# A fused attention and expert kernel: two rings for cluster scores, later casts, a later assignment for batch 1, and another bank in the opening

## The chip, the cores and the metric

The kernel runs on one core of a Trainium2 chip. The metric is the time of one execution on the device in microseconds (us); most executions agree within 0.3%. PE is the matrix engine, DVE the vector engine, ACT the scalar engine, POOL the engine called GpSimd, SP the engine whose queue issues most transfers. A profile is one execution; its span, from the first to the last instruction, is some 1.8 us shorter than the time.

## The reference, cut to what matters

```python
q_n, k_n, c_n = (x / (norm(x) + 1e-6) for x in (q, k, centroids))
q_assign = argmax(einsum('bhsd,hcd->bhsc', q_n, c_n), -1)     # 16 clusters a head
k_assign = argmax(einsum('bhsd,hcd->bhsc', k_n, c_n), -1)
mask = q_assign[:, :, :, None] == k_assign[:, :, None, :]
attn = softmax(where(mask, scale * q @ k.T, -1e9)) @ v         # (4, 8, 768, 64)
x = attn.transpose(0, 2, 1, 3).reshape(3072, 512)
p = domain_probs / (domain_probs.sum(-1, keepdims=True) + 1e-9)
for e in range(4):
    out += p[:, e:e+1] * (maximum(x @ w1[e], 0) @ w2[e])
```

Every query and every key of a head is assigned to its nearest cluster. A query attends to the keys of its own cluster. The result goes through four dense experts whose outputs are summed with weights.

## The kernel before: the parts that matter here

PE's instruction order is fixed by the program. Attention is cut into steps (24 to a unit of query rows, 72 to a batch), and the expert matmuls are woven between them. A third strand assigns the next batch to clusters: raw keys and queries are turned to have the head dimension on partitions, scored against the centroids, turned back, and the best cluster's one-hot row is written beside the keys and queries. This third strand is a list of numbered items, doled out over a stretch of steps, at most one item at each place where the experts yield.

```python
PS_BUFS = {"s": 2, "av": 1, "av2": 1, "mo": 3, "misc": 1}      # eight PSUM banks in rings
...
class Paced:                                   # items of a strand, spread over steps
    def run(self, step):
        if self.done < min(self.n, (step - self.at) * self.n / (self.to - self.at)):
            self.done += 1
            next(self.gen, None)
...
def assigns(b):                                # (keys, queries) of heads 0-3, then of heads 4-7
    xs = [Crossed(b, t, g, (("misc",), ("mo",))[t == 0])
          for t, g in ((1, 0), (0, 0), (1, 1), (0, 1))]
    for y, x in enumerate(xs):
        z = y % 2                              # 0: keys, 1: queries
        ...                                    # batch 1 is turned on PE, batches 2 and 3 by transfers
            put(t + 15, x.casts)               # DVE: fp32 to bf16 (t = 8 * y)
            at = 16 * (y // 2) + 24
        ...
        put(at, lambda x=x: x.scores_split("mo"))   # PE into "mo", then four DVE copies
...
# an expert: ph = bank("mo") four times (L728, emptied by ACT), then for each half of its rows
po = bank("mo")[:, c]                          # L747
nc.vector.scalar_tensor_tensor(oacc[:, c], po, pap, oacc[:, c], ...)   # L756, empties po
...
k1.turn(2, act)                                # the opening: last two turns of keys,
k1.turn(3, dve)                                # in "misc" and in "s" (attention's own ring)
...
at_step = {1: lambda: (puts(k0, 1), qa.put_narrow(slice(2, HG), "dve"), casts(k1, (1,))), ...}
...
for b in range(1, B):
    gens.append(Paced(assigns(b), XSTEPS[b], PER_B * (b - 1) if b > 1 else S1 + 4,   # S1 = 28
                      PER_B * b - 2))                                                # PER_B = 72
```

A tile takes a free bank of its ring, which is one whose last reader stands earlier in the program; PE then waits until that reader has run.

The softmax here doesn't subtract the row's maximum and nothing guards it: scores larger than these inputs give would overflow.

Of the kernel before, what the change touches and what calls it, by code (L numbers as in the profile page):

```python
# [20 lines left out]
def kernel(  # L21
# [27 lines left out]
    HG = H // 2  # L49
# [24 lines left out]
    act, dve, pool = nc.scalar.copy, nc.vector.tensor_copy, nc.gpsimd.tensor_copy  # L74
# [35 lines left out]
    def late(t, b):  # L110
        x = KF[b % 2].rearrange("p h r c -> p (h r c)")
        n = NP * A * 128
        return x[:, t * n:(t + 1) * n].rearrange("p (x i r c) -> p x i r c", i=QT, r=2, c=128)
# [28 lines left out]
    def load_raw(n=1, upto=len(ORDER)):  # L142
        for _ in range(n):
            if loaded < upto:
                load_part(*take_raw())

    def cast_v(b, g, js=range(HG)):
        for j in js:
            pool(VX[b % 2][:, g * HG + j, :, :D],
                 raw[b, 2, g][:, j, :].rearrange("p (a d) -> p a d", d=D))  # L150

    def load_w(e):
        nc.gpsimd.dma_start(out=W1[e], in_=moe_w1[e].rearrange("(i p) f -> p i f", p=128))
        nc.gpsimd.dma_start(out=W2[e], in_=moe_w2[e].rearrange("(i p) f -> p i f", p=128))
# [57 lines left out]
    class Assign:  # L212
# [104 lines left out]
        def put(self, j, r, on):  # L317

            p0 = 2 * CL * j
            self.move(self.rows(slice(D, D + CL), j, r),  # L320
                      self.ot[p0:p0 + CL, r * self.w:(r + 1) * self.w], on)
# [22 lines left out]
    class Crossed(Assign):  # L344
# [38 lines left out]
        def casts(self):  # L383
            y = self.g * HG // 2
            if self.b < ROWS:
                for r in range(2):
                    dve(self.rows(slice(0, D), slice(0, HG), r),
                        self.all[D * r:D * r + D, :].rearrange("p (j c) -> p j c", j=HG))
                return
            dve(late(self.t, self.b)[:, y:y + HG // 2], self.rows_of())  # L390
# [67 lines left out]
    def assigns(b):  # L458


        xs = [Crossed(b, t, g, (("misc",), ("mo",))[t == 0])
              for t, g in ((1, 0), (0, 0), (1, 1), (0, 1))]
        todo = {}

        def put(at, *fs):
            todo.setdefault(at, []).extend(fs)

        def turn(x, j):
            x.turn(j, dve)
            for r in range(2):  # L470
                x.cast(j, r, pool)

        for y, x in enumerate(xs):
            z = y % 2
            if b == 1:
                t = 12 * (y // 2) + 4 * z
                for j in range(HG):
                    put(t + j, lambda x=x, j=j: turn(x, j))
                put(t + 3, lambda: load_raw(upto=13))
                at = 12 * (y // 2) + 8  # L480
            else:
                t = 8 * y
                for j in range(HG):
                    put(t + j, lambda x=x, j=j: x.split(j))
                    put(t + 2 + j, lambda x=x, j=j: x.cross(j))
                    put(t + 9 + j, lambda x=x, j=j: x.merge(j))
                put(t + 6, load_raw)
                put(t + 15, x.casts)
                at = 16 * (y // 2) + 24
            if b == 1:  # L490
                put(at, lambda x=x: x.scores(dve))
                put(at + 1 + z, x.back, x.top, x.scale_onehot, x.cross_onehot)
                put(at + 4 + z, x.send_all)
                continue
            put(at, lambda x=x: x.scores_split("mo"))
            put(at + 2 + 6 * z, x.cross_scores)
            put(at + 5 + 6 * z, x.merge_scores)
            if b < ROWS:
                put(at + 9 + 6 * z, x.top, x.scale_onehot, x.cross_onehot)
                put(at + 13 + 6 * z, x.send_all)  # L500
                continue
            put(at + 9 + 6 * z, x.top, x.number, x.cross_numbers)
            put(at + 12 + 6 * z, x.store_numbers)
            put(at + 14 + 6 * z, x.spread_numbers)
        for g in range(2):
            if b == 1:
                put(1 + 18 * g, lambda g=g: load_w(2 + g))
                put(26 + 3 * g, lambda g=g: cast_v(b, g), lambda: load_raw(upto=13))
            else:
                for j in range(HG):  # L510
                    put(36 + 8 * g + j, lambda g=g, j=j: cast_v(b, g, (j,)))
                put(40 + 8 * g, load_raw)
        for at in range(XSTEPS[b]):
            for f in todo.pop(at, []):
                f()
            yield
        assert not todo
# [253 lines left out]
    PER_B = UB * PER_U  # L771
    LEAD = 6
    XSTEPS = [0, 31, 63, 63]
    step = 0
    gens = []
# [20 lines left out]
    k0, k1 = Assign(0, 1, 0, ("s", "mo", "mo", "mo")), Assign(0, 1, 1, ("s", "misc"))  # L796
    qa, qb = Assign(0, 0, 0, ("av",), 0, 1), Assign(0, 0, 1, ("mo",), 0, 1)
# [23 lines left out]
    k0.put(0, 1, "act")  # L821
    qa.onehot_narrow()
    qa.put_narrow(slice(0, 2), "dve")
    k1.turn(2, act)
    k1.turn(3, dve)
    k1.tags = ("mo", "misc")
    cast_v(0, 0)
# [17 lines left out]
                             dpr[:, :, None].broadcast_to([128, B * A, E]))  # L845

    psb = None
    def puts(x, j):
        for r in range(2):
            x.put(j, r, "dve")  # L850

    def late_casts():
        for j in range(HG):
            cast_v(0, 1, (j,))
            if j < 2:
                casts(k1, (2 + j,))

    at_step = {
        1: lambda: (puts(k0, 1), qa.put_narrow(slice(2, HG), "dve"), casts(k1, (1,))),
        2: lambda: (qb.turn(0, dve, True), puts(k0, 2)),  # L860
        3: lambda: (k1.scores(act), qb.scores(dve), puts(k0, 3)),
        5: lambda: (k1.back(), k1.top(), qb.back(), qb.top(),
                    qb.cast(0, 0, pool), qb.cast(0, 1, pool), late_casts()),
# [28 lines left out]
    S1 = PER_U + PAUSE  # L892
    gens.append(Paced(late_queries(), 5, S1 - 6, S1 + 4))
    for b in range(1, B):
        gens.append(Paced(assigns(b), XSTEPS[b], PER_B * (b - 1) if b > 1 else S1 + 4,
                          PER_B * b - 2))

    def woven(works, upto):

# [51 lines left out]
```

## Time and profile before

| | before |
|---|---|
| median time (3 runs) | 482.76 us |
| span of the profile | 480.9 us |
| busy: PE, ACT, DVE, POOL | 97%, 58%, 47%, 39% |
| PE idle in 0 to 72 us | 6.03 us |
| PE idle in 140 to 182 us | 2.99 us |
| PE idle in 256 to 294 us | 0.87 us |

The engine that sets the time is PE. The instructive question is not how busy it is but at which instructions it waited, and for whom. The profile answers that in the list of waits, and the timeline then shows what the engine waited for was doing. The prediction below prints these lines.

### The profile page before, as it was taken

Reading aid. Unit: us, or ns where it says so; the run is one execution under the profiler, and the core shown is the slowest. Engines: PE = TensorE matmul, PEld = TensorE weight load, DVE = VectorE, ACT = ScalarE, POOL = GpSimd, SP = SyncE. Lnnn points to the kernel's source line nnn. Section 1 sums busy time; section 2 is a strip of 40 time slices with the busy share of each in tenths; the row PEclk is TensorE's granted clock in tenths of the full one; section 3 lists DMA queues with packets and bytes.
Section 4 is the critical chain, followed back from the end, with each engine's and each line's share of the span. In section 5 each row is a group of like instructions: output and inputs, shape, how many; then the busy total and the mean of one; then the engine's idle time right before and its main releaser. Section 6 shows DMA issues by size and latency. Waiting matters only on the chain.

```text
span 480.9 us, 11389 instructions
## 1 busy us (share of the span) xinstructions
PE 467.7 (97%) x4539; PEld 332.6 (69%) x4539; DVE 226.7 (47%) x561; ACT 277.4 (58%) x502; POOL 186.2 (39%) x301
## 2 busy tenths in 40 slices
PE   8998999999999989999999999999999999999997
PEld 4776777677775657767766776777666666766675
DVE  5864664222324562422234444431877867765112
ACT  5755656555564546656655665566566585574341
POOL 5937479273343667180145834000313222221000
PEclk9999999999999999999999999999999999999999
DMA  8999953824564743614565573312000100100101
GB/s 281 254 211 347 237 106 54 152 57 127 92 131 111 159 102 81 143 34 51 140 140 110 119 135 115 87 35 75 27 29 13 50 14 7 34 30 10 46 2 44
DMA packets 74557, 48.01 MB, mean 100 GB/s; under 512 B 50248, under 2 KB 69256, under 8 KB 74504
## 3 DMA queue, kind: packets, MB, share of 16 engines
q1 hardware_dynamic: 65256, 37.96, 31.8%
q0 software_dynamic: 8576, 9.25, 10.8%
q8 instruction: 35, 0.57, 0.5%
q10 hardware_dynamic: 672, 0.08, 0.1%
q14 instruction: 18, 0.15, 0.1%
HBM read 37.31 MB, written 6.30 MB: 91 GB/s over the span
## 4 chain that ended last, share of the span: by engine, by line
PE 85%; DMA 5%; DVE 3%; SPq 3%; POOL 2%; issue 1%; ACT 0%; POOLq 0%; DVEq 0%; ACTq 0%
PE ps_mo L728 32%; PE ps_mo L747 31%; PE ps_s L638 8%; PE ps_av L665 7%; DMA raw<-in_k_dram 4%; SPq L368 1%; PE ps_s L548 1%; DMA sct<-scs 1%; SPq L336 1%; PE ps_misc L242 1%; POOL t L377 1%; PE ps_mo L400 1%; PE ps_mo L242 1%; PE ps_misc L548 1%; DVE oacc L756 1%
## 5 line engine op out<-in xcount | busy, mean ns | idle before, releaser
L644 ACT ACTIVATE at<-ps_s 128x512 bf16<-128x512 f32 x252 | 147.9, 595 | 125.7 <-PE ps_s L638 110.5
L728 PE MATMUL ps_mo<-xT,w1b 128*128 128x256 bf16 (+1 forms) x1664 | 195.7, 264 | 0.0
L747 PE MATMUL ps_mo<-w2b,hT 128*128 128x512 bf16 (+1 forms) x776 | 189.9, 377 | 2.8 <-DVE oacc L756 2.8
L728 PEld LDWEIGHTS <-w1b 128*128 128x128 bf16 x1664 | 146.3, 98 | 24.1 <-issue 0.6
L734 ACT ACTIVATE hT<-ps_mo 128x512 bf16<-128x512 f32 x192 | 114.7, 598 | 60.7 <-PE ps_mo L728 57.6
L756 DVE SCALAR_TENSOR_TENSOR oacc<-ps_mo,psb,oacc 128x512 f32<-128x512 f32 (+1 forms) x73 | 54.2, 742 | 125.5 <-PE ps_mo L747 125.3
L747 PEld LDWEIGHTS <-hT 128*128 128x128 bf16 x776 | 67.2, 98 | 61.4 <-issue 6.6
L638 PE MATMUL ps_s<-qf,kf 80*128 80x256 bf16 (+1 forms) x456 | 82.8, 267 | 0.7 <-DVE t L252 0.4
L665 PEld LDWEIGHTS <-at 128*128 128x128 bf16 x1152 | 69.9, 97 | 15.3 <-issue 1.7
L665 PE MATMUL ps_av<-vx,at 128*128 128x65 bf16 x1152 | 80.3, 193 | 0.0
L651 POOL TENSOR_TENSOR at<-at,same 128x512 bf16<-128x512 bf16 x24 | 28.2, 1176 | 97.7 <-ACT at L644 82.2
L638 PEld LDWEIGHTS <-kf 80*128 80x128 bf16 x456 | 42.4, 98 | 20.7 <-issue 1.6
L565 DVE TENSOR_SCALAR same<-qf,late 128x256 bf16<-128x256 bf16 x144 | 39.1, 324 | 0.0
L377 POOL COPY t<-t 128x768 uint16<-128x768 uint16 x32 | 35.6, 1119 | 0.3 <-DMA t<-h 0.3
L651 DVE TENSOR_TENSOR at<-at,same 128x512 bf16<-128x512 bf16 x48 | 21.6, 451 | 25.9 <-ACT at L644 25.8
L358 POOL COPY h<-raw 128x768 uint16<-128x768 uint16 x16 | 13.0, 826 | 37.2 <-DMA raw<-in_q_dram 31.0
L754 DVE TENSOR_SCALAR oacc<-ps_mo,psb 128x512 f32<-128x512 f32 x18 | 13.5, 750 | 28.5 <-PE ps_mo L747 28.5
L361 POOL COPY h<-raw 128x768 uint16<-128x768 uint16 x16 | 13.0, 825 | 33.0 <-DMA raw<-in_q_dram 19.5
L336 POOL DMA_DIRECT2D kf<-oht x32 | 16.4, 526 | 22.9 <-DMA oht<-oh 14.2
L416 POOL COPY st<-sct 128x384 uint16<-128x384 uint16 x16 | 9.9, 662 | 37.5 <-DMA sct<-scs 37.2
L672 DVE RECIPROCAL zr<-ps_av 128x4 f32<-128x4 f32 (+1 forms) x50 | 8.9, 178 | 30.1 <-PE ps_av L665 30.0
L674 DVE TENSOR_TENSOR xn<-ps_av,zr 128x256 bf16<-128x256 f32 (+1 forms) x50 | 20.7, 414 | 1.7
(127 smaller groups left out, 284.8 us busy)
## 6 DMA issues: line engine op xcount, KB each, us to landing
raw<-in_v_dram SPq DMA_DIRECT2D x8, 768.0 KB, 5.6
out_dram<-oacc SPq DMA_DIRECT2D x23, 256.0 KB, 2.0
raw<-in_k_dram SPq DMA_DIRECT2D x7, 768.0 KB, 6.6
raw<-in_q_dram SPq DMA_DIRECT2D x6, 768.0 KB, 4.9
w1b<-in_moe_w_dram POOLq DMA_DIRECT2D x4, 1024.0 KB, 11.8
w2b<-in_moe_w_dram POOLq DMA_DIRECT2D x4, 1024.0 KB, 17.1
qf<-nos SPq DMA_DIRECT2D x2, 768.0 KB, 4.0
xT<-xn SPq DMA_TRANSPOSE x72, 2.4
```

The costliest lines, as they stand in the source:

```text
L336: (nc.gpsimd if self.b or self.i0 and self.g else nc.sync).dma_start(out=self.rows(slice(D, D + CL), j, r), in_=self.oht[p0:p0 + CL, :self.w])
L377: pool(self.all[:, y * w:(y + 1) * w].bitcast(U16)[:, z::2], self.t16[:, (2 * z + y) * w:(2 * z + y + 1) * w])
L565: nc.vector.tensor_scalar(same[:, x * 256:(x + 1) * 256], clusters(b)[:, g, w, k // 2, k % 2, :], key_nos[b % 2][:, g, 8 * i + 4 * (k // 2 ...
L638: nc.tensor.matmul(sp[:, x * n:(x + 1) * n], KF[b % 2][:K, h, r, i * 128:(i + 1) * 128], QF[b % 2][:K, h, rs[0]:rs[-1] + 1, w * 128:(w + 1 ...
L644: nc.scalar.activation(at, sp, ACT.Exp, scale=scale)
L651: (nc.gpsimd if n4 in POOL_STEPS else nc.vector).tensor_tensor(at, at, same_cluster(b, w, cur), op=ALU.mult)
L665: nc.tensor.matmul(av[:, h % 2, m, :], at[:, c0:c0 + 128], VX[b % 2][:, h, 2 * i + r, :], start=(first and x == 0 and m == 0), stop=(last ...
L674: nc.vector.tensor_tensor(xn[:, :nr].rearrange("p i j d -> p j i d"), av[:, :, :, :D], zr.broadcast_to([128, 2, nr, D]), op=ALU.mult)
L728: nc.tensor.matmul(ph[:, x * n:(x + 1) * n], W1[e][:, i, (f + x) * 128:(f + x + 1) * 128], xT[:, i, :], start=(i == 0), stop=(i == ND - 1))
L734: nc.scalar.activation(ht, ph, ACT.Relu)
L747: nc.tensor.matmul(po, hT[f // per][:, c0:c0 + 128], W2[e][:, f, c], start=(f == 0), stop=(f == NF - 1))
L756: nc.vector.scalar_tensor_tensor(oacc[:, c], po, pap, oacc[:, c], op0=ALU.mult, op1=ALU.add)
```

## The change

Its intent is to keep the third strand out of the way of PE and of the ring "mo".

```diff
-                put(t + 15, x.casts)
+                put(t + 15 + 4 * z, x.casts)
...
-            put(at, lambda x=x: x.scores_split("mo"))
+            put(at, lambda x=x, t=("mo", "misc")[z]: x.scores_split(t))
...
     k1.turn(2, act)
+    puts(k0, 1)                       # head 1's one-hot rows, on DVE
+    k1.tags = ("av2",)
     k1.turn(3, dve)
...
-        1: lambda: (puts(k0, 1), qa.put_narrow(slice(2, HG), "dve"), casts(k1, (1,))),
+        1: lambda: (qa.put_narrow(slice(2, HG), "dve"), casts(k1, (1,))),
...
-        gens.append(Paced(assigns(b), XSTEPS[b], PER_B * (b - 1) if b > 1 else S1 + 4,
-                          PER_B * b - 2))
+        gens.append(Paced(assigns(b), XSTEPS[b], PER_B * (b - 1) if b > 1 else S1 + 7,
+                          PER_B * b - (2 if b > 1 else -2)))
```

No instruction is added or taken away.

More of the change, by code (lines that the diff above doesn't have):

```diff
@@ L823, with puts @@
     qa.put_narrow(slice(0, 2), "dve")
+    def puts(x, j):
+        for r in range(2):
+            x.put(j, r, "dve")
     k1.turn(2, act)
+    puts(k0, 1)
+    k1.tags = ("av2",)
     k1.turn(3, dve)
@@ L847 @@
     psb = None
-    def puts(x, j):
-        for r in range(2):
-            x.put(j, r, "dve")
     def late_casts():
```

## The prediction

> **What bounds the kernel now.** I read the page first: one core, span 480.9 us, granted clock nine tenths or more in all 40 slices, and a matrix engine (PE) that is busy nearly always.
>
> ```profile
> PE 467.7 (97%) x4539; PEld 332.6 (69%) x4539; DVE 226.7 (47%) x561; ACT 277.4 (58%) x502; POOL 186.2 (39%) x301
> ```
>
> No other engine is above 58%. So the time is PE's work plus PE's holes, and the change adds or removes no matmul. The question is which holes it closes. Second came busy time by stretches of the span (columns: us, then busy time of PE, weight loads, DVE, ACT, POOL, clock, DMA share, GB/s).
>
> ```profile
> 0.00:72.00 72.00, 65.97 (x798) 50.69 (x799) 45.75 (x129) 43.34 (x81) 44.20 (x89) 1.00 1.00 240
> 72.00:140.00 68.00, 68.00 (x665) 49.53 (x665) 20.78 (x40) 37.97 (x67) 33.27 (x75) 1.00 0.50 102
> 140.00:182.00 42.00, 39.01 (x368) 26.78 (x366) 22.44 (x38) 22.00 (x40) 26.13 (x34) 1.00 0.58 131
> ...
> 256.00:294.00 38.00, 37.13 (x347) 25.26 (x346) 20.13 (x36) 20.54 (x37) 19.82 (x24) 1.00 0.57 121
> ```
>
> PE stands idle 6.03 us in the first 72, 2.99 us in 140 to 182 and 0.87 us in 256 to 294. In the stretches between, and up to 440, its busy time is the whole stretch, so nothing later can absorb or return what is saved: a hole closed is time saved. Third came PE's own waits (total, times, longest), which name the holes.
>
> ```profile
> PE ps_mo L747 <- DVE oacc L756: 2.8, 2, 2.0
> PE ps_misc L242 <- DMA raw<-in_k_dram: 2.0, 2, 1.6
> ...
> PE ps_mo L400 <- DVE oacc L756: 1.0, 1, 1.0
> PE ps_misc L242 <- DVE t L252: 0.5, 2, 0.3
> PE ps_s L638 <- DVE t L252: 0.4, 1, 0.4
> ```
>
> L747 is the second matmul of an expert, L756 the DVE instruction that empties its bank, L400 the cluster scores of batches 2 and 3, L242 a transposition of raw keys or queries. Last, the timeline around each: batch 2's two score pairs, batch 3's second, then the opening and the first keys of batch 1 (start, duration, instruction, in brackets PE's wait).
>
> ```profile
> 145.32 1.92 DVE L387 CAST qf<-t 64x1536 bf16<-64x1536 f32 x2 [3.63 <-POOL t L377]
> 147.27 0.75 DVE L756 SCALAR_TENSOR_TENSOR oacc<-ps_mo,psb,oacc 128x512 f32<-128x512 f32 x1
> 148.17 0.85 PE L400 MATMUL ps_mo<-t,bdc 128*32 128x384 f32 x8 [1.00 <-DVE oacc L756]
> ...
> 176.07 2.22 DVE L387 CAST qf<-t 64x1536 bf16<-64x1536 f32 x2
> 178.32 0.75 DVE L756 SCALAR_TENSOR_TENSOR oacc<-ps_mo,psb,oacc 128x512 f32<-128x512 f32 x1
> 179.13 1.02 PE L747 MATMUL ps_mo<-w2b,hT 128*128 128x512 bf16 x4 [1.98 <-DVE oacc L756]
> ...
> 289.39 1.13 DVE L390 CAST kf<-t 128x1536 bf16<-128x1536 f32 x1
> 290.44 0.73 DVE L756 SCALAR_TENSOR_TENSOR oacc<-ps_mo,psb,oacc 128x512 f32<-128x512 f32 x1
> 291.22 1.02 PE L747 MATMUL ps_mo<-w2b,hT 128*128 128x512 bf16 x4 [0.87 <-DVE oacc L756]
> ```
>
> ```profile
> 12.67 0.56 DVE L252 COPY t<-ps_s 128x384 f32<-128x384 f32 x1 [0.38 <-PE ps_s L242]
> 13.28 0.38 PE L638 MATMUL ps_s<-qf,kf 80*128 80x256 bf16 x2 [0.43 <-DVE t L252]
> 15.09 0.16 PEld L267 LDWEIGHTS ps_mo<-t32q,bdc 128*32 128x32 f32 x8 [0.56 <-DVE t32q L252]
> ...
> 41.13 0.52 PE L242 MATMUL ps_misc<-ident,raw 128*128 128x128 f32 x3 [1.62 <-DMA raw<-in_k_dram]
> ```
>
> The pattern of the first three is one: DVE casts queries ahead of emptying an expert's bank, the two scores have just taken two of the three banks of "mo", and PE needs the bank that DVE has not emptied.
>
> **What the Trainium skill says.** "Perfetto Trace Analysis", section Identifying the Most-Contended Engine, warns that matmul busy time is no measure of the distance to the roofline because matmuls are pipelined; so I use PE's waits, not its 97%. The trace agrees: 1664 L728 matmuls have a mean of 264 ns, but eight of them take 0.87 us from start to start. Section Matmuls of the same page asks that independent matmul groups rotate through different PSUM banks, so that the emptying of one overlaps the next; here three banks rotate and the wait is one of 1.98 us. "VectorE: DVE Perf Modes", section The perf-mode tier table, gives an fp32 copy in SBUF at most two elements a cycle at 0.96 GHz. 1536 elements would be 0.80 us plus a fixed part; the trace has 0.96 us a cast (1.92 for two) and 1.11 beside POOL casts. "PSUM — Partial Sum Buffer", section Specifications (TRN2), has eight banks; the kernel's rings (2, 1, 1, 3, 1) use them all, so a bank can only be borrowed, which is what the change does.
>
> **The change part by part.** No instruction is added or removed.
>
> (a) Scores of queries go to "misc". At 148.17 the queries' scores no longer ask for the bank of the expert's first half: saves the 1.00 us wait. At 179.13 and 291.22 the second half of the expert no longer meets a ring with two score banks in it; it takes the bank of the last L728 group, emptied by ACT long before: saves 1.98 and 0.87 us. "misc" is free then: batch 1's assignment is over, and batch 3's attention, which uses it, starts later.
>
> (b) Query casts four work items later (one item is 70/63 of an attention step; an expert of six steps took about 9 us, so four items are about 6.6 us). Before, they sat one item ahead of the scores; now three behind. Worked through the expert's cost table, item 27 falls after the third L728 group and item 43 in the third, some 3 us ahead of the next first half's end, and a pair takes 1.92 to 2.22 us. So DVE is free again in time. (a) and (b) attack the same 1.00 + 1.98 + 0.87 = 3.85 us; I count it once. I take 3.8.
>
> (c) Batch 1 later: its items run from step 35 instead of 32, by the cost table at the seventh yield of that expert instead of the fourth. PE reached the keys at 41.13 - 1.62 = 39.5; three yields without transpositions cost about 0.77 us each (41.49 to 42.26), so it now arrives near 41.8, or 41.4 if the opening gains 0.4. The keys landed at about 41.0. Wait gone: 1.6 us, though with a margin of half a microsecond only. The "misc" ring's two short DVE waits (0.5 together) sit in the same crowded start; with one item a yield they may go or come back: I count 0.3. The end of batch 1's work moves from step 70 to 74, still before its attention at step 76, in a slow stretch where weights for 128-row units fill PE.
>
> (d) Opening. The last turn of keys leaves the two-bank "s" ring, so attention's second step no longer waits 0.43 us for DVE. Head 1's two writes (0.62 us) go into DVE's idle 0.38 us before that turn's copy, so the copy ends near 13.5 instead of 13.23; its new bank is first wanted by the first product with V at about 13.8. The next queue on DVE (the query copy ending at 15.03) comes about 0.38 us sooner, and PE's next wait (15.09) with it. I count 0.4, not 0.4 twice: it is one chain.
>
> Sum: 3.8 + 1.6 + 0.3 + 0.4 = 6.1 us, or 1.3%. 482.76 - 6.1 = 476.7.
>
> **Rivals.** First, a DVE queue that still decides: the moved casts land ahead of another emptying, or the scores' own copies (L404, four in 1.94 us) take the casts' place. For: DVE is busy 7.60 of 10 us around 172 to 182. Against: program order puts the emptying (L756) ahead of L404, and PE would have 1.4 us of score matmuls to cover it. If it holds, half of 3.8 is lost: about 478.6. Second, the keys of batch 1 are still late, or bunching of shifted items brings new ring waits: for it, DMA's share is 1.00 over the first 72 us, and the next keys and queries land only at 45.6 and 47.9. Then (c) is worth 0.6 and the time is about 477.8; in a bad case with new waits it gives all back, 478.6. Third, the opening's gain is swallowed by a later DMA or ACT wait before 41: 477.1. Fourth, a better spacing clears the remaining small waits of the first 72 us as well: PE's waits on DVE there (0.5, 0.4, 0.3) would add 0.5 to 1: near 475.8.
>
> **Range and chances.** Both of the first two rivals together give 479.5 to 480.5, which I hold for less likely than one in ten; the fourth gives the low end. Range 475.0 to 479.3. A gain over 2% needs 9.7 us, more than all the waits concerned (3.85 + 1.6 + 0.5 + 0.4 and some neighbours), and there is no plausible 9.7 us loss: 2% faster, 97% within, 1% slower.
>
> **What would show it.** Right: PE's waits on L756 before L747 and L400 vanish; stretches around the three scores are all PE; the wait on raw keys is under 0.3 us apart from 0.4 us before 10 us; query casts start two or three experts' groups after the scores; attention's second step follows the first by about 0.35 us in place of 0.81. Wrong: a new PE wait on DVE L252 or L404 of over 1 us between 40 and 72, or after the casts' new place; or a span that shrinks less than the waits do, which would mean the holes were not additive.

## The result

The changed kernel takes 475.5 us (median of 4 runs, 475.39 to 476.3) where the kernel before took 482.66 us in the same rounds (482.14 to 483.82). The ratio is 0.9852, with a 95% interval of 0.9831 to 0.9873. Ratios here are the mean time of one kernel's fast runs over that of the other's fast runs of the same rounds, so they aren't quite the ratio of the medians. The changed kernel's four had a granted clock of 0.999 or 1.0. The medians differ by 7.16 us, the spans of the two profiles by 7.3 us. The kernel is faster beyond the noise, but by less than 2%.

The page's line of busy times, after:

```profile
PE 464.2 (98%) x4488; PEld 333.2 (70%) x4539; DVE 227.1 (48%) x561; ACT 277.1 (59%) x502; POOL 187.8 (40%) x301
```

PE has 4488 matmul records here and 4539 before, with 4539 weight loads in both: 51 matmul records are missing from this trace, so PE's busy time reads low, and I place instructions by weight loads below. Busy time by the same stretches as before, after the change (the columns are those of the prediction's view):

```profile
0.00:72.00 72.00, 68.53 (x825) 53.74 (x831) 46.10 (x129) 46.12 (x86) 44.49 (x89) 1.00 1.00 240
72.00:140.00 68.00, 67.52 (x657) 49.86 (x665) 21.10 (x41) 37.54 (x67) 37.17 (x80) 1.00 0.52 108
140.00:182.00 42.00, 41.73 (x388) 28.84 (x392) 22.89 (x39) 24.24 (x44) 27.27 (x37) 1.00 0.58 129
256.00:294.00 38.00, 37.79 (x352) 26.94 (x355) 20.15 (x36) 22.25 (x40) 19.62 (x26) 1.00 0.61 125
```

PE's idle time fell from 6.03 to 3.47 us in the first 72, and from 2.99 to 0.27 in 140 to 182. The rest of 0.2 to 0.5 us a stretch is the missing records: the second stretch, which had no hole before and has no named wait now, shows 0.48. PE's waits, after (total, times, longest):

```profile
PE ps_s L87 <- DVE blank L80: 1.2, 1, 1.2
PE ps_mo L276 <- ACT scs L271: 0.4, 1, 0.4
PE ps_misc L296 <- DVE oh L287: 0.4, 2, 0.2
...
PE ps_s L638 <- DMA kf<-oht: 0.2, 1, 0.2
```

All five waits that the prediction showed are gone from this list: both kinds on L756, the one on raw keys, and both on L252. The first line is the start of the kernel. The last one, attention waiting for the transfer of head 6's one-hot rows, isn't in the list of the kernel before; but it is also in those of e1_bank, e2_casts, e3_both, e4_later and f3_no_open below (0.2 to 0.4 us), whose opening is unchanged, so the change didn't bring it. The timeline after, at the scores of batch 2's first half, the casts of that half, the scores and casts of its second half, and the second scores of batch 3:

```profile
143.21 0.85 PE L400 MATMUL ps_mo<-t,bdc 128*32 128x384 f32 x8
...
149.30 2.44 DVE L387 CAST qf<-t 64x1536 bf16<-64x1536 f32 x2
...
171.75 0.73 DVE L756 SCALAR_TENSOR_TENSOR oacc<-ps_mo,psb,oacc 128x512 f32<-128x512 f32 x1
172.01 0.83 PE L400 MATMUL ps_misc<-t,bdc 128*32 128x384 f32 x8
172.78 1.04 PE L747 MATMUL ps_mo<-w2b,hT 128*128 128x512 bf16 x4
...
177.62 1.92 DVE L387 CAST qf<-t 64x1536 bf16<-64x1536 f32 x2
...
283.95 1.04 PE L747 MATMUL ps_mo<-w2b,hT 128*128 128x512 bf16 x4
```

L400 and L747 have no wait in brackets. The emptying (L756) ran while PE was at the scores, and the casts are now 5 to 6 us behind the scores. Last, the opening and batch 1's first keys, after:

```profile
12.43 0.62 DVE L315 TENSOR_SCALAR kf<-ps_mo 16x384 bf16<-16x384 bf16 x2
12.58 0.60 PE L638 MATMUL ps_s<-qf,kf 80*128 80x256 bf16 x4
13.08 0.56 DVE L252 COPY t<-ps_av 128x384 f32<-128x384 f32 x1
...
41.21 0.52 PE L242 MATMUL ps_misc<-ident,raw 128*128 128x128 f32 x3
```

Attention's first two steps are now one run of four matmuls, and the first turn of raw keys has no wait.

**Where the time came from.** I paired the weight loads of the two traces in order, for each kind of weights, and took the difference of their start times. It grows in few places. It is 0.46 us from 27.2 to 38.7 us, 3.10 from 77.7 (after jumps while items exchange places), 4.31 from 149.0, 6.34 from 179.1 and 7.26 from 291.2, and stays there to the end (times of the kernel before). So the stretch of the opening gave 0.46, batch 1's strand 2.64, and the three score groups 1.21, 2.03 and 0.92 us. In between, nothing was lost or won.

### The profile page after: what moved, and what is told of

The parts are those of the page before. It is cut to its first block, busy times and chain, and to the rows that moved or that the text cites. A ratio compares the mean times of both kernels' runs of the same rounds, so it can differ in the third digit from the quotient of the medians.

```text
span 473.6 us, 11333 instructions
## 1 busy us (share of the span) xinstructions
PE 464.2 (98%) x4488; PEld 333.2 (70%) x4539; DVE 227.1 (48%) x561; ACT 277.1 (59%) x502; POOL 187.8 (40%) x301
## 4 chain that ended last, share of the span: by engine, by line
PE 96%; DVE 1%; issue 1%; ACT 1%; ACTq 0%
PE ps_mo L728 35%; PE ps_mo L747 34%; PE ps_s L638 10%; PE ps_av L665 8%; PE ps_s L548 1%; PE ps_mo L242 1%; PE ps_misc L242 1%; PE ps_misc L548 1%; PE ps_s L87 1%; PE ps_mo L267 1%; PE ps_mo L400 1%; PE ps_misc L267 1%; PE ps_misc L400 1%; DVE oh L287 0%; DVE mx L284 0%
## 5 line engine op out<-in xcount | busy, mean ns | idle before, releaser
L747 PE MATMUL ps_mo<-w2b,hT 128*128 128x512 bf16 (+1 forms) x725 | 186.2, 377 | 2.3
L756 DVE SCALAR_TENSOR_TENSOR oacc<-ps_mo,psb,oacc 128x512 f32<-128x512 f32 (+1 forms) x73 | 54.1, 742 | 127.0 <-PE ps_mo L747 122.5
L747 PEld LDWEIGHTS <-hT 128*128 128x128 bf16 x776 | 67.0, 98 | 57.5 <-issue 3.1
L336 POOL DMA_DIRECT2D qf<-oht x40 | 20.1, 510 | 4.5 <-DVE oht L313 3.9
```

The costliest lines, as they stand in the source:

```text
L336: (nc.gpsimd if self.b or self.i0 and self.g else nc.sync).dma_start(out=self.rows(slice(D, D + CL), j, r), in_=self.oht[p0:p0 + CL, :self.w])
L747: nc.tensor.matmul(po, hT[f // per][:, c0:c0 + 128], W2[e][:, f, c], start=(f == 0), stop=(f == NF - 1))
```

## The experiments

All twelve kernels gave correct results. Two quantities from the traces serve throughout, because they are steadier than the times. One is the time from attention's first step (its first weight load) to its fourth; the first step itself starts anywhere from 12.35 to 13.23 us and shifts all that follows. (The loads aren't the reason, for each of raw keys, queries and values in the first 12 us lands within 0.3 us of the same moment in all profiles. What differs is PE's pace: its first turns of raw keys follow each other every 0.21 us, later ones every 0.11, and this changes at 4.6 us in the kernel before, near 5.8 in the changed one and near 7.2 in f2_no_ahead. Across the fourteen traces, the later it changes, the later is the first step, but for ties of 0.01 to 0.02 us.) The other is the time from the first turn of batch 1's keys to the end.

### The scores' bank and the casts (three runs, run together, 3 rounds)

e1_bank does the bank alone:

```diff
-            put(at, lambda x=x: x.scores_split("mo"))
+            put(at, lambda x=x, t=("mo", "misc")[z]: x.scores_split(t))
```

> Only the bank of the query scores of batches 2 and 3 changes. Theory (a ring that asks for a bank DVE has not emptied makes the three holes): all three waits on L756 (1.00, 1.98, 0.87 us) vanish although the casts still stand ahead of L756 on DVE, and the kernel gains 3.9 to 4.3 us: about 478.5. Rival 1 (the order on DVE makes the holes, the bank only decides who waits): the wait comes back at the next L728 group or at the scores, and the gain is under 2 us. The stretches 140 to 182 and 256 to 294 decide it.

e2_casts does the casts alone:

```diff
-                put(t + 15, x.casts)
+                put(t + 15 + 4 * z, x.casts)
```

> Only the query casts move four items later, all scores stay in mo. Theory (either cure alone is enough, because L756 then runs before PE asks for the bank): the same 3.9 to 4.3 us, about 478.5, with at most 0.2 us of waits on L756 left. Rival 2 (with both scores in mo the ring is one bank short whatever DVE does): the waits at the second score pairs stay at 0.8 us or more each, gain under 2.5 us.

e3_both does both edits, and nothing else of the change:

> Bank and casts together, nothing else. Theory: the two cure the same holes, so the gain is that of either alone within 0.3 us (about 478.5), not the sum. Rival: the two gain separately, and both together gain 1 us or more over the better of the two.

| kernel | median us (4 runs) | ratio to before, 95% interval | first turn of keys to the end |
|---|---|---|---|
| before | 482.39 (7 runs) | | 439.81 |
| e1_bank | 478.21 | 0.9908, 0.9886 to 0.9930 | 435.61 |
| e2_casts | 478.24 | 0.9910, 0.9888 to 0.9932 | 435.59 |
| e3_both | 478.46 | 0.9914, 0.9887 to 0.9941 | 435.70 |

(Before's last column is from its one profile, at another time.) Each edit alone gains 4.2 us, and both together gain no more. The theory holds and all three rivals fall. The timelines show that the two cure the same hole in different ways. First e1_bank, then e2_casts, at the scores of batch 2's second half:

```profile
174.37 2.22 DVE L387 CAST qf<-t 64x1536 bf16<-64x1536 f32 x2
175.51 1.04 PE L747 MATMUL ps_mo<-w2b,hT 128*128 128x512 bf16 x4
176.62 0.75 DVE L756 SCALAR_TENSOR_TENSOR oacc<-ps_mo,psb,oacc 128x512 f32<-128x512 f32 x1
```

```profile
174.59 0.73 DVE L756 SCALAR_TENSOR_TENSOR oacc<-ps_mo,psb,oacc 128x512 f32<-128x512 f32 x1
175.25 1.93 DVE L404 COPY scs<-ps_mo 128x384 uint16<-128x384 uint16 x4
175.52 1.04 PE L747 MATMUL ps_mo<-w2b,hT 128*128 128x512 bf16 x4
```

With the other bank, DVE is as late as ever: the emptying starts at 176.62, behind the casts, and PE has gone ahead at 175.51 because it needs another bank. With the casts moved, PE needs the same bank as before, but the emptying was over at 175.32, 0.2 us before PE came. A late engine and a short ring made the hole together, and taking away either closed it.

### Batch 1 later (three runs)

e4_later (3 rounds, beside the three above) is the changed start and end alone:

```diff
-... S1 + 4, PER_B * b - 2))
+... S1 + 7, PER_B * b - (2 if b > 1 else -2)))
```

> Only batch 1's assignment is later (from step 35, to step 74). Theory: it removes the wait on keys (1.6 to 1.8 us) and also the two short holes at 45.54 (0.51) and 59.93 (0.34), 2.6 us in all: about 480.0. Rival (only the DMA wait counts, the short holes went by other parts of the change): 1.6 to 1.8 us, about 481.0, and waits of L242 on DVE L252 stay.

It took 479.7 us (479.04 to 479.85), ratio 0.9937 (0.9914 to 0.9960). By paired weight loads it is 0.06 us ahead at 38 us and 2.70 from 77.7: 2.64, the theory's 2.6, so all three holes went by this part. PE's waits on raw keys and on L252 in turns of batch 1 are gone, and those on L756 are still there.

Then two half measures, later, with 3 rounds. e8_later_part starts one yield later instead of three, and keeps the new end; e9_end_only keeps the old start and takes the new end:

```diff
-... S1 + 7, ...        # e8_later_part: S1 + 5; e9_end_only: S1 + 4
```

> The kernel before with batch 1's assignment from step 35 replaced by from step 33 (one yield later than before instead of three), end at step 74. Theory (the keys land at 40.6 to 41.0 whatever the issue, and each yield is about 0.77 us of PE work that fits into the wait): PE still starts its first turn about 0.1 us after the landing, with a wait that is about 0.77 us shorter than in a kernel before of the same start; gain 0.8 us, up to 1.6 if the short holes go as well. Rival (later items make the load later too, or any delay is as good as three yields): the wait stays at its length, or is gone altogether.

> The kernel before with only the end of batch 1's assignment moved, from step 70 to 74; its start stays at step 32. Theory (spacing of items makes the two short holes, the start makes the wait on keys): the wait on keys stays (first turn 0.1 us after the landing), the hole of 0.51 us at 45.5 goes because the fourth turn of keys now falls one yield later; gain 0.4 to 0.9 us. Rival (the start alone matters): within 0.1 us of before from the landing on.

e8_later_part took 482.65 us (481.84 to 483.6), ratio 1.0015 (0.9997 to 1.0032); e9_end_only 483.13 us (480.53 to 484.82), ratio 1.0018 (0.9978 to 1.0058). Neither gained what was expected. For e9_end_only the interval alone would still hold a gain of 0.4 to 0.9 us; the traces decide: by paired weight loads, between 38 and 80 us, e8_later_part won 0.14 us and e9_end_only lost 0.09. (Two of e8_later_part's runs were at 0.996; the two at full clock took 481.84 and 481.97, where the kernel before had a median of 481.99.) What they said of the start and of the hole at 45.5 us came true: in e8_later_part the wait on keys is 0.67 us where it was 1.62, and in e9_end_only the hole at 45.5 is gone and PE is 1.05 us ahead at 58.5. But both then lose it in a new hole. In e9_end_only:

```profile
58.60 0.26 DVE L426 TENSOR_SCALAR oh<-oh 128x384 bf16<-128x384 bf16 x1
58.98 0.42 DVE L674 TENSOR_TENSOR xn<-ps_av,zr 128x256 bf16<-128x256 f32 x1
59.46 0.29 PE L681 MATMUL ps_mo<-identb,xn 128*128 128x128 bf16 x2 [1.04 <-DVE xn L674]
```

L681 turns attention's output. From 55.4 to 59.4 us DVE works without a pause through the best clusters of keys and queries (1.4 us each) and the emptying of an expert, and only then comes to this output. In the kernel before, the output was ready at the same time, 59.40 us, but PE, being later, met it without a wait. So the gain ran into DVE. In the changed kernel the same work falls one yield further on, and the output of attention passes ahead of it (xn at 54.79, best clusters from 55.28). The rival of e8_later_part (the wait stays, or is gone) fell too. So it isn't enough that batch 1 is somewhat later; it matters where its items fall between the experts' yields. One half measure was not run: the start three yields later with the old end. Whether the new end is needed at all stays open.

### The opening (four runs, run together, 5 rounds; 4 to 6 runs a kernel)

e5_open has only the opening's two edits on the kernel before. The other three start from the changed kernel: f3_no_open undoes both, f1_no_bank only the bank, f2_no_ahead only head 1's place.

```diff
 # f1_no_bank
-    k1.tags = ("av2",)
 # f2_no_ahead
-    puts(k0, 1)
-        1: lambda: (qa.put_narrow(slice(2, HG), "dve"), casts(k1, (1,))),
+        1: lambda: (puts(k0, 1), qa.put_narrow(slice(2, HG), "dve"), casts(k1, (1,))),
```

> Only the opening's two edits on the kernel before. Theory (the keys of batch 1 landed at 40.6 to 41.0 us in all six traces so far, although their issue moved from 32.8 to 33.9, so PE meets a wall there that the opening doesn't move): PE reaches the keys 0.3 to 0.5 us sooner, waits that much longer (1.9 to 2.1 instead of 1.62), and the time gains at most 0.2 us. Rival (the prediction's sum, in which the 0.4 us stand by themselves): 0.4 us, about 482.0, with the wait on keys unchanged.

> The changed kernel with both edits of the opening undone. Theory: with the wait on keys gone there is no wall, so the opening is worth its full 0.3 to 0.5 us: about 475.9 where the changed kernel has 475.5. Rival: worth nothing here either, 475.5.

> The changed kernel, the last turn of keys back in ring s, head 1 still ahead of it. Theory (the bank is what frees the second step; head 1's writes of 0.62 us now delay the copy that empties the bank): the second step waits 0.6 to 0.8 us for DVE instead of 0.43, and the time is 0.3 to 0.7 us above the changed kernel. Rival (the order on DVE is what gains): within 0.1 us of the changed kernel.

> The changed kernel, the bank kept, head 1's writes back behind the copy. Theory (the copy of the queries on DVE ends where it did before, near 15.03, and PE waits for it with the query scores): 0.15 to 0.4 us above the changed kernel, most of the opening's gain lost. Rival (the bank alone gives it all): within 0.1 us.

| kernel | median us | ratio to before, 95% interval | step 1 to step 4 | first turn of keys | landing of these keys |
|---|---|---|---|---|---|
| before | 483.01 (11 runs) | | 3.08 | 41.10 | 41.00 |
| after (another time) | 475.5 | 0.9852 | 2.75 | 41.18 | 40.69 |
| e5_open | 482.49 | 0.9990, 0.9965 to 1.0014 | 2.75 | 40.77 | 40.66 |
| f3_no_open | 476.38 | 0.9856, 0.9835 to 0.9878 | 3.08 | 41.50 | 40.76 |
| f1_no_bank | 476.54 | 0.9859, 0.9837 to 0.9880 | 3.27 | 41.73 | 40.66 |
| f2_no_ahead | 476.36 | 0.9855, 0.9833 to 0.9877 | 3.08 | 42.74 | 40.56 |

The times can't tell effects of a third of a microsecond: the three undone kernels agree within 0.2 us, and the changed kernel was not run beside them, so its 475.5 is compared through the ratios only, whose intervals overlap. The traces can. The fourth step follows the first after 3.08 us in every trace without the opening's edits and after 2.75 us in every trace with both: 0.33 us. The bank alone gives nothing (3.08), and head 1 ahead without the bank loses 0.19 us (3.27). The two edits work only together. In f1_no_bank the copy that frees the bank comes later than ever; in f2_no_ahead the copy of the queries is as late as before and PE waits for it:

```profile
13.12 0.56 DVE L252 COPY t<-ps_s 128x384 f32<-128x384 f32 x1
13.69 0.38 PE L638 MATMUL ps_s<-qf,kf 80*128 80x256 bf16 x2 [0.69 <-ACT at L644]
```

```profile
15.21 0.69 DVE L252 COPY t32q<-ps_mo 128x512 f32<-128x512 f32 x1
15.96 0.32 PE L267 MATMUL ps_mo<-t32q,bdc 128*32 128x128 f32 x4 [0.27 <-DVE t32q L252]
```

(In f1_no_bank the profile names ACT as the releaser. ACT's instruction ended at 13.64 and DVE's copy at 13.68, so I read the copy, the later of the two, as what PE waited for.) f2_no_ahead reached its first step 0.76 us later than the changed kernel (PE's slower first turns, above), and lost another 0.5 us to the transfer for head 6 (a wait of 0.7), so its first turn is late by more than its edit.

e5_open shows the wall that its theory named: PE starts on the keys 0.11 us after they land, as in the kernel before (0.10), in e1_bank, e2_casts, e3_both, e8_later_part and e9_end_only (0.10 to 0.11). The landing doesn't follow the issue: in all fourteen traces the keys landed between 40.55 and 41.00 us, although they were issued between 32.59 and 34.09. So whatever the opening gains is waited away there, unless batch 1 comes later. The size of the wait was missed (1.31 us where I had said 1.9 to 2.1), because this profile's first step came at 12.84 us instead of 12.36, so that PE was at the keys no sooner (39.5 in both), and because its keys landed 0.34 us sooner. That an opening alone is worth nothing in time agrees with its ratio of 0.9990, but the interval would also hold 0.4 us; the evidence is the wall in the traces.

### Two attempts to go further (5 rounds)

y1_send_first moves one transfer ahead of DVE work in the changed kernel; y2_gap adds an empty item to the late queries of batch 0.

```diff
-        7: lambda: (k1.onehot(2), puts(k1, 0), k1.keep(), k1.send_all((2, 3))),
+        7: lambda: (k1.onehot(2), k1.keep(), k1.send_all((2, 3)), puts(k1, 0)),
 # y2_gap as well
         qd.top()
         yield
+        yield
         qd.onehot()
-    gens.append(Paced(late_queries(), 5, S1 - 6, S1 + 4))
+    gens.append(Paced(late_queries(), 6, S1 - 6, S1 + 6))
```

> The changed kernel with one more edit: in step 7 of the opening the writes for heads 6 and 7 are kept and sent before head 4's own writes (0.62 us of DVE). In the changed kernel PE waits 0.18 us at 26.09 for that transfer (0.7 in the run without head 1 ahead). Theory: the transfer lands 0.6 us earlier, the wait goes, gain 0.15 to 0.35 us over the changed kernel. Rival: head 4's writes or the query writes behind them are now late, and as much is lost.

> As y1_send_first, and an empty item between the best cluster and its one-hot turn in the late queries of batch 0, which PE meets right behind each other (a hole of 0.34 us at 37.19 in the changed kernel). Theory: this hole goes too, another 0.25 to 0.35 us. Rival: the query writes of heads 4 to 7 now land after attention wants them (step 40), and PE waits there as much or more.

y1_send_first took 475.52 us (475.24 to 476.36), ratio 0.9869 (0.9854 to 0.9884), and y2_gap 475.79 us (475.08 to 476.73), ratio 0.9873 (0.9858 to 0.9887). Neither is clearly better or worse than the changed kernel. The named waits did go: the transfer for head 6 in both, the one at 37 us in y2_gap. From step 1 to the first expert matmul y1_send_first needs 16.16 us where the changed kernel needs 16.26, so its gain is 0.1 us and not 0.15 to 0.35; a wait for attention's output (L681, now 0.4 us) took the rest. And its profile gives back some 0.35 us more at the scores of batch 2's second half, where PE now waits for POOL's last copy of turned queries, which ends at 172.12:

```profile
169.80 2.32 POOL L377 COPY t<-t 128x768 uint16<-128x768 uint16 x2
172.17 0.14 PEld L400 LDWEIGHTS ps_misc<-t,bdc 128*32 128x32 f32 x4 [0.23 <-POOL t L377]
```

f3_no_open loses some 0.3 us in the same way, which isn't the opening's own. In the changed kernel this copy ends at 171.72 and PE loads the weights made from it at 171.77, so there is no margin left: POOL is the next engine to watch there. In y2_gap PE reaches the keys at 40.89 us, 0.10 us after their landing at 40.79: it stands at the wall again. By paired weight loads its profile still ends 0.29 us ahead of the changed kernel's, which its runs (475.08 to 476.73) can't confirm. A faster opening would now need batch 1 later still, or its keys earlier.

## Why the prediction was right

The measured 475.5 us lies in the range of 475.0 to 479.3, 1.2 us below the 476.7 predicted. By the prediction's own parts:

- **(a) and (b), counted once, 3.8 us.** Right in mechanism, and the counting once is shown: 4.20 us for the bank alone, 4.22 for the casts alone, 4.11 for both (differences of the last column of the first table). The size is low: in the changed kernel the three places gave 1.21 + 2.03 + 0.92 = 4.16 us, where the waits read 1.00 + 1.98 + 0.87. The step that was mis-sized is "saves the 1.00 us wait": by paired weight loads that place gave 1.21, in e1_bank, e2_casts and e3_both too. The likely reason is that PE's idle time is counted from the modelled end of its last matmul, and in a full pipeline the next one starts long before that end (L747: 0.38 us recorded, 0.22 from start to start).
- **(c) 1.6 + 0.3 us.** Right in mechanism and wrong in size: 2.64 us in the changed kernel, and in e4_later. The step that failed is "they may go or come back: I count 0.3". Both short holes went, and counted from start to start the three holes were 1.78, 0.51 and 0.34 us, 2.63 in all. The doubt itself was sound: in e8_later_part and e9_end_only a new hole of 1.2 us did come. Some of the size is chance: the keys of the one profile before landed at 41.00, later than in any other, and the wait would have read less with another landing (1.44 us in e9_end_only, at 40.76). Arrival was forecast at 41.4 with a margin of half a microsecond, and was 41.18 with 0.49.
- **(d) 0.4 us.** The chain that the prediction drew is what the traces show: 0.33 us from step 1 to step 4, through the bank and the earlier copy of the queries together. That the whole stretch gives 0.46, close to 0.4, is partly chance: e4_later and f3_no_open, whose opening is unchanged, lead by 0.06 and 0.15 us at the same place. And "a hole closed is time saved" does not hold for it by itself: in the kernel before, the wait on keys 26 us later takes it all. It counts only because (c) removes that wait.
- **The sum.** 4.16 + 2.64 + 0.46 = 7.26 us against 6.1. There was no loss from any part, and no later stretch gave anything back.

Of the rivals, the first (DVE still decides) did not come about. The second (late keys or new ring waits) is false of the change but true of its halves. The third (the opening swallowed before 41 us) is true on the kernel before and false on the changed one. The fourth, a better spacing that clears the small waits too, is the nearest to what happened, though its arithmetic was only a guess: two of the three waits that it adds (0.5 and 0.4) were already counted in (c) and (d). In the second, 477.8 should read 478.0 (476.7 with 0.6 in place of 1.9). The 0.80 us for a cast is an estimate; the traces have 0.96. Of the signs named, the waits, the stretches, the place of the casts and the raw keys' wait came as said. Attention's second step follows the first by about 0.22 us (four matmuls without a break, of which two fill 0.226 us) and not 0.35.

What the traces don't settle is why the keys land at the same time whatever the issue. That the 16 transfer engines are full then (their share reads 1.08 of the time from 0 to 40 us in the changed kernel) suggests a backlog, but no run here took it away.

## What to carry to other kernels

When one engine is nearly always busy, list its waits, and for each ask for both causes: the buffer it needs and the engine that is late; either can be cured, and one cure is enough. Add gains only after asking what the next wait downstream is: a stretch that ends at a landing transfer gives back whatever was won ahead of it. After moving items of a woven strand, look again at what now falls beside them: both half moves tried here put other work in front of attention's output and gained next to nothing.

## What the Trainium skill lacked or had wrong

- "Perfetto Trace Analysis", section Per-engine timelines, says that the end of a matmul in the profile is an estimate. It doesn't say what follows for waits: an idle time counted from that end came out short of the time that its removal gained, 1.00 us against 1.21 at one place, and 1.62 + 0.5 against 2.64 for batch 1's first stretch.
- The same page, section Optimization Strategy, has one look for a gap and make its dependency faster. In this case two unrelated cures closed the same gaps (4.20 and 4.22 us, 4.11 together), and one part's gain vanished at a later landing; I found no place there that warns of adding gaps up.
- No page that I read has it that a load's landing may not move with its issue: 768 KB loads issued from 32.59 to 34.09 us landed from 40.55 to 41.00.
